# Linear attention beside softmax attention on one core: the start-up order, the guard's last operations and a new table for the order of work

## The chip, the cores and the metric

One core of a Trainium2 chip runs the whole program. The metric is the device time of one execution in microseconds; the time of a kernel is the median of several executions. A separate execution is profiled, and its span runs from the first to the last recorded instruction, so it is a little shorter than that execution's device time.

## The reference

Two independent attention blocks, A and B, each on 2048 tokens of width 512 with 32 heads of 16. A is linear attention with the feature map phi, B is full softmax attention. Their outputs lie side by side in the last dimension.

```python
def _A_ref(x, wqkv, wo):
    q, k, v = ...                       # x @ wqkv, 32 heads of 16
    phi = lambda t: jnp.where(t > 0, t + 1, jnp.exp(t)) + 1e-6
    pq, pk = phi(q), phi(k)
    kv = jnp.einsum("bhsd,bhse->bhde", pk, v)
    z = jnp.einsum("bhsd->bhd", pk)
    num = jnp.einsum("bhqd,bhde->bhqe", pq, kv)
    den = jnp.einsum("bhqd,bhd->bhq", pq, z)[..., None] + 1e-6
    return (num / den) ... @ wo

def _B_ref(x, wqkv, wo):
    q, k, v = ...
    scores = jnp.einsum("bhqd,bhkd->bhqk", q, k) * Dh ** -0.5
    o = jnp.einsum("bhqk,bhkd->bhqd", softmax(scores, axis=-1), v)
    return o ... @ wo

return concatenate([a, b], axis=-1)     # bfloat16, 1 x 2048 x 1024
```

## The kernel before

**What the bulk of the work is.** Block B has 32 heads times 2048 by 2048 scores. The kernel cuts them into 32 units (`NU`: four groups of heads, four spans of 512 queries, and the even or odd heads of the group), and each unit into 64 blocks of 128 keys by 512 queries (`UB`), 2048 blocks in all. A block needs one score matmul on PE (`qk`, L871), an exponential, and the product with V (L1129). The exponential can be done in two ways. In the first, ACT does it: two or three blocks lie in a PSUM tile `pS`, and one ACTIVATE at L1048 writes them to `PT` in 16 bits; V is then multiplied once. In the second, DVE and POOL do it with integers: the block lies in one of two banks of the PSUM tile `pD`, DVE scales and shifts it into an integer that read as a 16-bit float is close to the exponential (L956, tile `DI`), POOL adds two constants to it for two blocks at a time (L980), which makes two more shifted versions, and V is multiplied three times, with three scaled copies of V, so that the errors of the approximation cancel. This text calls the first an ACT block and the second a D block.

**Everything else** is inserted between: projections of B (`proj_job`, `v4_job`), the whole of block A (`akv_job`, `akvsum_job`, `aq_job`, `aden_job`, `anum_job`, `omm_job`), and the closing of each unit (`unit_done`).

**What sets the order.** All instructions of the four engines lie in one fixed order, which a planner in the Python program works out when the kernel is built. It keeps a planned time for each engine (`T`), a list of ready candidates with planned durations, and takes at each step the candidate with the earliest planned start; near ties go by priority, to which a random number from a seeded generator may be added. Nineteen parameters steer it, `NAMES`; one row of the table `POLICY` holds their values for 8 us of planned PE time (`SEG`), and there are 86 rows. `DBL`, the eighth, bounds the planned backlog of DVE and POOL above which no further D block is taken; `AQ`, the eighteenth, holds back the exponentials of block A; `SEED` is the fifteenth. How many of the 2048 blocks become D blocks is no constant: it comes out of this process. Dependencies between engines become semaphore waits (`Sched.add`), derived from named resources that each operation reads and writes.

**The port's turn.** A resource named `"PORT"` keeps some operations of DVE and POOL from overlapping. POOL's operations at L980 and L1191 read it; some DVE operations with two SBUF inputs write it (the phi stages at L699 and L700, the V copies at L686). Each side waits for the other's semaphore. In the plan such an operation is marked as locked, from the `keys` of its function, and starts only when POOL is planned to be free. `both` makes one planned operation of several instructions and takes the `keys` of the first.

**The guard.** `flag_job` (from L650) bounds the largest possible score: three small reductions, three matmuls, one reduction (L661), and then three operations on single numbers, L663 to L665, that leave a flag in `FLG`. The flag decides whether a general softmax has to run, which it does not for these inputs. In the plan each of the three is 0.1 us long and not locked, and none writes `"PORT"`.

**The denominators of A.** `aden_job` (from L743) plans two halves of eight matmuls at 0.0625 us for each.

**The start.** Before the planner begins, an order written by hand runs: 28 warm-up matmuls (L1206), then for each of the first four token tiles a transpose on PE (four matmuls, L570, into bank t of `SBANKS`) and a copy to `xTb` (L563, by DVE for tiles 0 and 2, by ACT for 1 and 3). The two x loads for tiles 0, 1 and 2, 3 are issued on the SP and the ACT queue. `first_proj` (L1219) is a projection for half a span, 256 tokens, of four matmuls; `first_k` (L1224) writes its result into `KM` for even or odd heads. The first half of K (bank `SBANKS[4]`) is projected in the loop, after tile 1 and before the transposes of tiles 2 and 3; then follow the two halves of Q (banks of `pD`, copies at L1237 and L1239) and the second half of K. After that the planner takes over from fixed planned times (`T` is 7.8, DVE 8.9).

Of the kernel before, what the change touches and what calls it, by code (L numbers as in the profile page):

```python
# [13 lines left out]
ALU = mybir.AluOpType  # L14
# [218 lines left out]
def bass_concat_heads__linear_attn_block__softmax_full_mha__prompt_kernel(nc, A_x, A_wqkv, A_wo, B_x, B_wqkv, B_wo, out):  # L233
# [7 lines left out]
    SC = 0.25  # L241
# [13 lines left out]
        (0.15, 3.5, 4.2, 0, 3, 5, 32, 3.0, 1.0, 16, 10.0, 0.0, 0, 0, 633, 1, 0.0, 0.0, 2.0),  # L255
        (0.05, 3.5, 4.2, 0, 3, 4, 32, 3.0, 1.0, 16, 10.0, 0.0, 1.5, 0, 0, 1, 0.0, 0.0, 2.0),
        (0.15, 3.5, 4.2, 0, 3, 5, 32, 3.0, 1.0, 16, 10.0, 0.0, 0, 0, 275, 1, 0.0, 0.0, 2.0),
        (0.05, 3.5, 4.2, 0, 3, 4, 32, 3.0, 1.0, 16, 10.0, 0.0, 1.5, 0, 0, 1, 0.0, 0.0, 2.0),
        (0.05, 3.5, 4.2, 0, 3, 4, 20, 3.0, 1.0, 16, 40.0, 0.0, 1.5, 0, 497, 1, 0.0, 0.0, 2.0),
        (0.15, 3.5, 3, 0, 3, 4, 32, 3.0, 1.0, 16, 10.0, 0.0, 0, 0, 503, 1, 0.0, 0.0, 2.0),  # L260
        (0.15, 3.5, 3, 0, 3, 4, 20, 3.0, 1.0, 16, 10.0, 0.0, 0, 0, 503, 1, 0.0, 0.0, 2.0),
        (0.15, 3.5, 4.2, 0, 3, 4, 32, 3.0, 1.0, 16, 10.0, 0.0, 0, 0, 0, 1, 0.0, 0.0, 2.0),
        (0.15, 3.5, 3, 0, 3, 4, 20, 3.0, 1.0, 16, 10.0, 0.0, 0, 0, 503, 1, 0.0, 0.0, 2.0),
        (0.15, 3.5, 4.2, 0, 3, 4, 32, 3.0, 1.0, 16, 10.0, 0.0, 0, 0, 0, 1, 0.0, 0.0, 2.0),
        (0.15, 3.5, 3, 0, 3, 4, 20, 3.0, 1.0, 16, 10.0, 0.0, 0, 0, 138, 1, 0.2, 0.0, 2.0),
        (0.15, 3.5, 3, 0, 3, 7, 20, 3.0, 1.0, 16, 10.0, 0.0, 0, 0, 313, 1, 0.2, 0.0, 2.0),
        (0.15, 3.5, 3, 0, 3, 7, 20, 3.0, 1.0, 16, 10.0, 0.0, 0, 0, 313, 1, 0.2, 0.0, 2.0),
        (0.15, 3.5, 3, 0, 3, 4, 32, 3.0, 1.0, 16, 10.0, 0.0, 0, 0, 155, 1, 0.0, 0.0, 2.0),
        (0.15, 3.5, 3, 0, 3, 4, 32, 3.0, 1.0, 16, 10.0, 0.0, 0, 0, 155, 1, 0.0, 0.0, 2.0),
        (0.15, 3.5, 4.2, 0, 3, 4, 32, 3.0, 1.0, 16, 10.0, 0.0, 0, 0, 0, 1, 0.0, 0.0, 2.0),  # L270
        (0.15, 3.5, 3, 0, 3, 4, 32, 3.0, 1.0, 16, 10.0, 0.0, 0, 0, 155, 1, 0.0, 0.0, 2.0),
        (0.15, 3.5, 3, 0, 3, 4, 32, 3.0, 1.0, 16, 10.0, 0.0, 0, 0, 9, 1, 0.0, 0.0, 2.0),
        (0.15, 2.05, 4.2, 0, 3, 4, 32, 3.0, 1.0, 16, 20.0, 0.0, 0, 0, 0, 1, 0.0, 0.0, 2.0),
        (0.15, 2.05, 4.2, 0, 3, 4, 32, 3.0, 1.0, 16, 20.0, 0.0, 0, 0, 222, 4, 0.0, 0.0, 2.0),
        (0.15, 3.5, 3, 0, 3, 4, 32, 3.0, 1.0, 16, 10.0, 0.0, 0, 0, 166, 1, 0.0, 0.0, 2.0),
        (0.15, 3.5, 3, 0, 3, 4, 32, 3.0, 1.0, 16, 10.0, 0.0, 0, 0, 166, 1, 0.0, 0.0, 2.0),
        (0.15, 3.5, 4.2, 0, 3, 4, 32, 3.0, 1.0, 16, 10.0, 0.0, 0, 0, 841, 1, 0.0, 0.0, 2.0),
        (0.15, 3.5, 4.2, 0, 3, 4, 32, 3.0, 1.0, 16, 10.0, 0.0, 0, 0, 625, 1, 0.0, 0.0, 2.0),
        (0.15, 3.5, 2.6, 0, 3, 4, 32, 3.0, 1.0, 16, 10.0, 0.0, 0, 0, 166, 1, 0.0, 2.0, 2.0),
        (0.15, 3.5, 2.6, 0, 3, 4, 32, 3.0, 1.0, 16, 10.0, 0.0, 0, 0, 166, 1, 0.0, 2.0, 2.0),  # L280
        (0.15, 3.5, 2.6, 0, 3, 4, 32, 3.0, 1.0, 16, 10.0, 0.0, 0, 0, 166, 1, 0.0, 2.0, 2.0),
        (0.15, 3.5, 2.6, 0, 3, 4, 32, 3.0, 1.0, 16, 10.0, 0.0, 0, 0, 166, 1, 0.0, 2.0, 2.0),
        (0.15, 3.5, 2.6, 0, 3, 4, 32, 3.0, 1.0, 16, 10.0, 0.0, 0, 0, 549, 1, 0.0, 2.0, 2.0),
        (0.15, 4.5, 2.6, 0, 3, 4, 32, 3.0, 1.0, 16, 40.0, 0.0, 0, 0, 889, 1, 0.0, 2.0, 2.0),
        (0.15, 3.5, 2.6, 0, 3, 4, 32, 3.0, 1.0, 16, 10.0, 0.0, 0, 0, 549, 1, 0.0, 2.0, 2.0),
        (0.15, 3.5, 4.2, 0, 3, 4, 32, 3.0, 1.0, 16, 10.0, 0.0, 0, 0, 0, 1, 0.0, 0.0, 0.3),
        (0.15, 3.5, 2.6, 0, 3, 4, 32, 3.0, 1.0, 16, 10.0, 0.0, 0, 0, 549, 1, 0.0, 2.0, 2.0),
        (0.15, 3.5, 4.2, 0, 3, 4, 32, 3.0, 1.0, 16, 10.0, 0.0, 0, 0, 0, 1, 0.0, 0.0, 2.0),
        (0.15, 3.5, 2.6, 0, 3, 4, 32, 3.0, 1.0, 16, 10.0, 0.0, 0, 0, 549, 1, 0.0, 2.0, 2.0),
        (0.15, 3.5, 4.2, 0, 3, 4, 32, 3.0, 0.2, 16, 10.0, 0.0, 0, 0, 916, 1, 0.0, 2.0, 2.0),  # L290
        (0.15, 3.5, 2.6, 0, 3, 4, 32, 3.0, 1.0, 16, 10.0, 0.0, 3, 0, 863, 1, 0.0, 2.0, 2.0),
        (0.15, 3.5, 2.6, 0, 3, 4, 32, 3.0, 1.0, 16, 10.0, 0.0, 3, 0, 13, 1, 0.3, 2.0, 2.0),
        (0.15, 2.5, 4.2, 0, 3, 4, 32, 3.0, 1.0, 16, 10.0, 0.0, 0, 0, 851, 1, 0.0, 0.0, 2.0),
        (0.15, 2.5, 4.2, 0, 3, 4, 32, 3.0, 1.0, 16, 10.0, 0.0, 0, 0, 851, 1, 0.0, 0.0, 2.0),
        (0.15, 3.5, 2.6, 0, 3, 4, 32, 3.0, 1.0, 16, 10.0, 0.0, 3, 0, 63, 1, 0.2, 2.0, 2.0),
        (0.15, 3.5, 2.6, 0, 3, 4, 32, 3.0, 1.0, 16, 10.0, 0.0, 3, 0, 63, 1, 0.2, 2.0, 2.0),
        (0.15, 3.5, 2.6, 0, 3, 4, 32, 3.0, 1.0, 16, 10.0, 0.0, 3, 0, 63, 1, 0.2, 2.0, 2.0),
        (0.15, 3.5, 2.6, 0, 3, 4, 32, 3.0, 1.0, 16, 10.0, 0.0, 3, 0, 172, 1, 0.2, 2.0, 2.0),
        (0.15, 3.5, 2.6, 0, 3, 4, 32, 3.0, 1.0, 16, 10.0, 0.0, 3, 0, 500, 1, 0.3, 2.0, 2.0),
        (0.15, 3.5, 4.2, 0, 3, 4, 32, 3.0, 1.0, 16, 10.0, 0.0, 0, 1.5, 820, 1, 0.0, 0.0, 2.0),  # L300
        (0.15, 3.5, 4.2, 0, 3, 4, 32, 3.0, 1.0, 16, 10.0, 0.0, 0, 1.5, 820, 1, 0.0, 0.0, 2.0),
        (0.15, 3.5, 2.6, 0, 3, 4, 32, 3.0, 1.0, 16, 10.0, 0.0, 3, 0, 1, 1, 0.3, 2.0, 2.0),
        (0.15, 3.5, 4.2, 0, 3, 4, 32, 3.0, 1.0, 16, 10.0, 0.0, 0, 0, 0, 1, 0.0, 0.0, 2.0),
        (0.15, 3.5, 6, 0, 2, 4, 32, 3.0, 1.0, 16, 10.0, 0.0, 3, 0, 1, 1, 0.3, 2.0, 2.0),
        (0.15, 3.5, 6, 0, 2, 4, 32, 3.0, 1.0, 16, 10.0, 0.0, 3, 0, 1, 1, 0.3, 2.0, 2.0),
        (0.15, 3.5, 4.2, 0, 3, 4, 32, 3.0, 1.0, 16, 10.0, 0.0, 0, 0, 530, 1, 0.0, 0.0, 0.3),
        (0.15, 3.5, 6, 0, 2, 4, 32, 3.0, 1.0, 16, 10.0, 0.0, 3, 0, 1, 1, 0.3, 2.0, 2.0),
        (0.05, 3.5, 6, 0, 2, 4, 32, 3.0, 1.0, 16, 10.0, 0.0, 3, 0, 525, 1, 0.3, 2.0, 4.0),
        (0.15, 3.5, 6, 0, 2, 4, 32, 3.0, 1.0, 16, 10.0, 0.0, 3, 0, 1, 1, 0.3, 2.0, 2.0),
        (0.15, 3.5, 2.6, 0, 2, 4, 32, 3.0, 1.0, 16, 10.0, 0.0, 3, 0, 996, 1, 0.3, 0.0, 2.0),  # L310
        (0.15, 3.5, 4.2, 0, 3, 4, 32, 3.0, 1.0, 16, 10.0, 0.0, 0, 0, 0, 1, 0.0, 0.0, 2.0),
        (0.15, 3.5, 4.2, 0, 3, 4, 32, 3.0, 1.0, 16, 10.0, 0.0, 0, 0, 0, 1, 0.0, 0.0, 2.0),
        (0.25, 3.5, 2.6, 0, 2, 4, 32, 6.0, 1.0, 16, 10.0, 0.0, 0.5, 0, 996, 1, 0.3, 0.0, 2.0),
        (0.25, 4.5, 2.6, 0, 2, 4, 32, 6.0, 0.2, 16, 10.0, 0.0, 0.5, 0, 996, 1, 0.0, 0.0, 2.0),
        (0.25, 4.5, 2.6, 0, 2, 4, 32, 6.0, 0.2, 16, 10.0, 0.0, 0.5, 0, 996, 1, 0.0, 0.0, 2.0),
        (0.25, 4.5, 2.6, 0.1, 2, 4, 32, 9.0, 1.0, 16, 10.0, 0.0, 0.5, 0, 684, 1, 0.3, 0.0, 2.0),
        (0.25, 4.5, 2.6, 0, 2, 4, 32, 6.0, 0.5, 16, 10.0, 0.0, 0.5, 0, 829, 1, 0.0, 0.0, 2.0),
        (0.25, 4.5, 2.6, 0.1, 2, 4, 32, 9.0, 1.0, 16, 10.0, 0.0, 1.5, 0, 883, 1, 0.3, 0.0, 2.0),
        (0.25, 4.5, 2.6, 0, 2, 4, 32, 6.0, 0.5, 16, 10.0, 0.0, 3, 0.5, 231, 1, 0.0, 0.0, 2.0),
        (0.25, 4.5, 2.6, 0, 2, 4, 32, 6.0, 0.5, 16, 10.0, 0.0, 3, 0.5, 231, 1, 0.0, 0.0, 2.0),  # L320
        (0.25, 4.5, 2.6, 0, 2, 4, 32, 6.0, 0.5, 16, 10.0, 0.0, 3, 0.5, 231, 2, 0.0, 0.0, 4.0),
        (0.25, 4.5, 2.6, 0, 2, 4, 32, 6.0, 0.5, 16, 10.0, 0.0, 3, 0.5, 231, 2, 0.0, 1.0, 4.0),
        (0.25, 4.5, 2.6, 0, 2, 4, 32, 6.0, 0.5, 16, 10.0, 0.0, 1.5, 0.5, 553, 1, 0.0, 0.0, 2.0),
        (0.25, 4.5, 2.6, 0, 4, 4, 32, 6.0, 0.5, 16, 10.0, 0.0, 3, 0.5, 231, 2, 0.0, 1.0, 4.0),
        (0.25, 4.5, 2.6, 0, 4, 4, 32, 6.0, 0.5, 16, 10.0, 0.0, 3, 0.5, 231, 2, 0.0, 1.0, 4.0),
        (0.15, 3.5, 3, 0, 3, 4, 32, 9.0, 1.0, 16, 10.0, 0.0, 0, 0, 0, 2, 0.0, 0.0, 2.0),
        (0.25, 4.5, 2.6, 0, 4, 4, 32, 6.0, 0.5, 16, 10.0, 0.0, 3, 0.5, 251, 2, 0.0, 1.0, 2.0),
        (0.15, 3.5, 3, 0.1, 3, 4, 32, 9.0, 1.0, 16, 10.0, 0.0, 0, 0, 0, 2, 0.45, 0.0, 2.0),
        (0.15, 3.5, 3, 0, 3, 4, 32, 9.0, 1.0, 16, 40.0, 0.0, 0, 0, 0, 2, 0.0, 0.0, 2.0),
        (0.25, 3.5, 3, 0, 3, 4, 32, 9.0, 1.0, 16, 40.0, 0.0, 0, 0, 701, 2, 0.0, 0.0, 2.0),  # L330
        (0.25, 3.5, 3, 0, 3, 4, 32, 9.0, 1.0, 16, 40.0, 0.0, 0, 0, 701, 2, 0.0, 0.0, 2.0),
        (0.5, 3.5, 3, 0, 3, 4, 32, 6.0, 1.0, 24, 40.0, 0.0, 0, 0, 0, 2, 0.0, 0.0, 2.0),
        (0.25, 3.5, 3, 0, 3, 5, 32, 9.0, 1.0, 16, 40.0, 0.0, 0, 0, 928, 2, 0.0, 0.0, 2.0),
        (0.15, 3.5, 4.2, 0, 3, 4, 32, 3.0, 1.0, 16, 10.0, 0.0, 0, 0, 259, 1, 0.0, 0.0, 2.0),
# [14 lines left out]
    with es:  # L349
# [25 lines left out]
        PQT = sb("PQT", [128, 1, 4, 512], BF)  # L375
# [852 lines left out]
        for t in range(4):  # L1228
# [4 lines left out]
            if t == 1:  # L1233
                first_proj(SBANKS[4], 1, 0)
# [304 lines left out]
```

## Time and profile before

| what | before |
|---|---|
| median of 6 runs | 704.26 us (701.69 to 704.92) |
| the profiled execution, device time | 703.66 us |
| its span | 701.8 us |
| mean granted TensorE clock | 0.998 |
| busy: PE, ACT, DVE, POOL | 666.2, 681.2, 573.1, 579.9 us |
| ACT blocks: ACTIVATEs on three and on two blocks | 291 and 290, which is 1453 blocks |
| D blocks: score matmuls into `pD` at L871 | 595 |
| POOL's operation for two D blocks, L980 | 1890 ns mean |
| first exponential (L1048) starts, last ends | 10.87 us, 692.96 us |

The times are microseconds from the first instruction. ACT is busy 97% of the span. A busy PE is not a PE at its peak, since the records of pipelined matmuls overlap. Device time and span of the profiled execution differ by 1.9 us; the span and the median by 2.5 us.

### The profile page before, as it was taken

The page shows a single profiled execution, that of the slowest core. Times are in us where ns is not written, and L with a number is a line of the kernel's source. Part 1 is how long each engine was busy: PE and PEld are TensorE (multiplying, and loading weights), DVE is VectorE, ACT ScalarE, POOL GpSimd, SP SyncE. Part 2 cuts the span into 40 slices and gives each one's busy share as a digit, 9 for nine tenths or more (in the row PEclk, how much of TensorE's full clock was granted, in tenths as well). Part 3 has the DMA queues.
Part 4 walks back from the last instruction along what each step waited for, and adds up shares of the span by engine and source line. Part 5 has one row for each costly group of instructions (what it writes and reads, how often), then busy time and mean ns, then how long its engine had stood idle before and what let it go on. Part 6 is the DMA issues. An engine that isn't in the chain of part 4 may idle for free.

```text
span 701.8 us, 15842 instructions
## 1 busy us (share of the span) xinstructions
PE 666.2 (95%) x6740; PEld 226.3 (32%) x6740; DVE 573.1 (82%) x1022; ACT 681.2 (97%) x637; POOL 579.9 (83%) x350
## 2 busy tenths in 40 slices
PE   7999998999999999999999999999999999999996
PEld 5333443333333334332222223332222222322221
DVE  4878889888788888888888888978889888887873
ACT  5799999999999999999999999999999999999995
POOL 6398666787888887896899879987789987998993
PEclk9999999999999999999999999999999999999999
DMA  9900000000000000010000000000010000101001
GB/s 208 243 1 3 2 1 4 8 14 9 2 2 1 2 1 2 1 40 16 18 23 23 9 1 16 24 24 9 15 30 18 16 16 25 24 23 38 17 24 34
DMA packets 35788, 17.34 MB, mean 25 GB/s; under 512 B 26496, under 2 KB 35200, under 8 KB 35712
## 3 DMA queue, kind: packets, MB, share of 16 engines
q1 hardware_dynamic: 34480, 15.48, 9.3%
q8 instruction: 55, 0.90, 0.5%
q10 hardware_dynamic: 1232, 0.79, 0.4%
q14 instruction: 21, 0.17, 0.1%
HBM read 4.72 MB, written 4.19 MB: 13 GB/s over the span
## 4 chain that ended last, share of the span: by engine, by line
ACT 80%; PE 11%; DVE 5%; POOL 3%; issue 0%; ACTq 0%; POOLq 0%
ACT PT L1048 77%; PE pPV L1129 4%; PE pS L871 2%; POOL DI L980 2%; ACT EA L697 2%; DVE DI L956 2%; PE pD L871 1%; PE pD L787 1%; PE pD L677 1%; PE pD L708 1%; PE pD L1206 0%; PE pD L595 0%; DVE KM L608 0%; DVE VV L686 0%; DVE KNa L700 0%
## 5 line engine op out<-in xcount | busy, mean ns | idle before, releaser
L1048 ACT ACTIVATE PT<-pS 128x1536 f16<-128x1536 f32 x581 | 667.6, 1337 | 5.9 <-PE pD L871 3.5
L980 POOL TENSOR_TENSOR DI<-DI,SHC 128x1024 int32<-128x1024 int32 x298 | 555.4, 1890 | 99.1 <-DVE DI L956 46.3
L956 DVE TENSOR_SCALAR DI<-pD 128x512 int16<-128x512 f32 (+1 forms) x588 | 391.8, 691 | 70.8 <-PE pD L871 59.4
L1129 PE MATMUL pPV<-DI,VV 128*17 128x512 f16 x1785 | 245.7, 381 | 0.9 <-DVE OT L1184 0.7
L1129 PE MATMUL pPV<-PT,VV 128*17 128x512 f16 x1453 | 241.5, 382 | 1.6 <-ACT PT L1048 1.1
L871 PE MATMUL pS<-QT,KM 32*128 32x512 bf16 x1453 | 226.0, 384 | 16.3 <-ACT PT L1048 11.3
L871 PE MATMUL pD<-QT,KM 32*128 32x512 bf16 x595 | 211.7, 384 | 5.1 <-DVE DI L956 3.6
L871 PEld LDWEIGHTS pS<-QT,KM 32*128 32x128 bf16 x1453 | 55.4, 91 | 193.5 <-ACT PT L1048 146.1
L1129 PEld LDWEIGHTS pPV<-DI,VV 128*17 128x17 bf16 x1785 | 52.4, 88 | 70.7 <-issue 52.2
L871 PEld LDWEIGHTS pD<-QT,KM 32*128 32x128 bf16 x595 | 51.5, 90 | 65.6 <-DVE DI L956 40.8
L1129 PEld LDWEIGHTS pPV<-PT,VV 128*17 128x17 bf16 x1453 | 51.6, 88 | 59.1 <-issue 42.8
L708 PE MATMUL pD<-Wa,xTa 128*128 128x128 bf16 x512 | 36.7, 220 | 1.1 <-DVE DI L956 0.8
L595 PE MATMUL pD<-xTb,Wb 128*128 128x512 bf16 x120 | 33.0, 383 | 0.4 <-DVE VV L682 0.2
L708 PEld LDWEIGHTS pD<-Wa,xTa 128*128 128x128 bf16 x512 | 28.8, 98 | 12.7 <-DVE DI L956 7.7
L1191 POOL TENSOR_TENSOR OT<-OT,ZR 128x256 bf16<-128x256 f32 x31 | 19.3, 621 | 10.3 <-DVE KNa L700 4.7
L1184 DVE STREAM_TRANSPOSE OT<-pPV 128x512 f32<-128x512 f32 x31 | 22.0, 709 | 2.7 <-PE pPV L1129 2.6
L677 PE MATMUL pD<-Wb,xTb 128*128 128x128 bf16 x256 | 18.5, 220 | 0.4 <-DVE DI L956 0.4
L711 DVE CAST KNa<-pD 128x256 bf16<-128x256 f32 x32 | 13.4, 419 | 6.5 <-PE pD L708 6.5
L735 PE MATMUL pD<-xTa,Wa 128*128 128x512 bf16 x64 | 17.8, 383 | 0.3 <-DVE DI L956 0.3
L787 PE MATMUL pD<-WOa,ONT 128*128 128x512 bf16 x64 | 18.0, 383 | 0.0
L697 ACT ACTIVATE EA<-KNa 128x256 bf16<-128x256 bf16 x32 | 15.4, 481 | 1.2 <-DVE KNa L711 1.2
L677 PEld LDWEIGHTS pD<-Wb,xTb 128*128 128x128 bf16 x256 | 14.4, 98 | 6.7 <-DVE DI L956 3.8
(106 smaller groups left out, 303.0 us busy)
## 6 DMA issues: line engine op xcount, KB each, us to landing
out_dram<-OB SPq DMA_DIRECT2D x16, 128.0 KB, 1.7
out_dram<-KNa SPq DMA_DIRECT2D x13, 128.0 KB, 1.7
Wa<-in_A_wqkv_dram SPq DMA_DIRECT2D x1, 1536.0 KB, 7.3
KM<-KR SPq DMA_DIRECT2D x96, 16.0 KB, 1.8
Wb<-in_B_wqkv_dram SPq DMA_DIRECT2D x2, 384.0 KB, 4.1
Wb<-in_B_wqkv_dram SPq DMA_DIRECT2D x1, 512.0 KB, 4.9
WOa<-in_A_wo_dram SPq DMA_DIRECT2D x1, 512.0 KB, 8.0
VNa<-in_B_wo_dram SPq DMA_DIRECT2D x1, 512.0 KB, 4.3
```

Of the source, the lines that this page charges most:

```text
L595: return e.matmul(f32v(bk), lhsT=Wb[:, cc, kind * 512 + Gp * 128:kind * 512 + Gp * 128 + 128], rhs=xTb[:, cc, sc * 512:(sc + 1) * 512], st ...
L677: return e.matmul(f32v(bk)[:, tl * 128:(tl + 1) * 128], lhsT=xTb[:, cc, t * 128:(t + 1) * 128], rhs=Wb[:, cc, 1024 + Gp * 128:1024 + Gp * ...
L697: ("act", 0.051 + n * 0.000833, f_op("act", lambda e: e.activation(EA[:, q, 0:n], t_ap, ACTF.Exp), list(keys), [("EA", q)])),
L708: return e.matmul(f32v(bk)[:, 128 * x:128 * x + 128], lhsT=xTa[:, cc, (t + i_) * 128:(t + i_ + 1) * 128], rhs=Wa[:, cc, c0:c0 + 128], star ...
L787: return e.matmul(f32v(bk), lhsT=src, rhs=WO[:, hb, :], start=(hb == 0), stop=(hb == 3))
L871: return e.matmul(dst, lhsT=KM[32 * g:32 * g + 32, Gp % 2, e_, j * 128:(j + 1) * 128], rhs=QT[32 * g:32 * g + 32, Gp % 2, c * 512:(c + 1) ...
L956: sch.add("dve", lambda e: e.tensor_scalar(DI[:, buf, 0, i * 512:(i + n) * 512], DB[:, bi * 512:(bi + n) * 512], ESC, EB, op0=ALU.mult, op ...
L980: sch.add("pool", lambda e: e.tensor_tensor(DI32[:, buf, 1:3, 0:w], DI32[:, buf, 0, 0:w].unsqueeze(1).broadcast_to([128, 2, w]), SHC32[:]. ...
L1048: sch.add("act", lambda e: e.activation(PT[:, row, c0:c0 + w], SCR[sl][:, 0:w], ACTF.Exp, scale=SC), reads=skeys(sl), writes=[("PT", row, ...
L1129: sch.add("pe", lambda e, g=g, vk=vk, c0=c0, P=P, first=first, last_=last_: e.matmul(PVb[32 * g:32 * g + 17, 0:512], lhsT=VV[:, Gp % 2, vk ...
L1184: sch.add("dve", lambda e: e.transpose(OT[:, 0, :], PVb[:, 0:512]), reads=[("PV", g) for g in range(4)], writes=[("OT", 0)])
L1191: (ml, 0.65, f_op(ml, lambda e: e.tensor_tensor(xn[:, :, 16 * e_:16 * e_ + 16], o[:, :, 0:16], zr.unsqueeze(2).broadcast_to([128, 16, 16]) ...
```

## The change

It has four parts. All four transposes of the start are issued before the first projection of half of K; before, that projection stood between the second and the third. The guard's last three operations become one planned operation of 0.5 us, each of them writes `"PORT"`, and so the whole is locked and each waits for POOL, and POOL for them. The planned duration of one matmul in `aden_job` is 0.03 us where it was 0.0625. And the table `POLICY` has 86 new rows; one row, by position, is the same as before, and the rows in which `DBL` is above 3.0 are 31 where they were 21.

```diff
     POLICY = [
-        (0.15, 3.5, 4.2, 0, 3, 5, 32, 3.0, 1.0, 16, 10.0, 0.0, 0, 0, 633, 1, 0.0, 0.0, 2.0),
-        (0.05, 3.5, 4.2, 0, 3, 4, 32, 3.0, 1.0, 16, 10.0, 0.0, 1.5, 0, 0, 1, 0.0, 0.0, 2.0),
...
         (0.15, 3.5, 4.2, 0, 3, 4, 32, 3.0, 1.0, 16, 10.0, 0.0, 0, 0, 0, 1, 0.0, 0.0, 2.0),
+        (0.25, 3.5, 4.2, 0, 3, 4, 20, 3.0, 1.0, 16, 10.0, 0.0, 0, 0, 0, 1, 0.0, 0.0, 1.0),
+        (0.25, 3.5, 3, 0, 3, 4, 20, 3.0, 0.5, 16, 10.0, 0.0, 0, 0, 0, 1, 0.0, 0.0, 1.0),
...
-                ("dve", 0.1, f_op("dve", lambda e: e.tensor_tensor(GR1[:, 3:4], GR1[:, 1:2], GR1[:, 2:3], op=ALU.mult), ["GR1"], ["GR2"])),
-                ("dve", 0.1, f_op("dve", lambda e: e.scalar_tensor_tensor(GR1[:, 2:3], GR1[:, 0:1], SC * SC, GR1[:, 0:1], op0=ALU.mult, op1=ALU.mult), ["GR1", "GR2"], ["GR1"])),
-                ("dve", 0.1, f_op("dve", lambda e: e.tensor_tensor(FLG[:], GR1[:, 3:4], GR1[:, 2:3], op=ALU.mult), ["GR1", "GR2"], ["FLG"]))],
+                ("dve", 0.5, both(
+                    f_op("dve", lambda e: e.tensor_tensor(GR1[:, 3:4], GR1[:, 1:2], GR1[:, 2:3], op=ALU.mult), ["GR1"], ["GR2", "PORT"]),
+                    f_op("dve", lambda e: e.scalar_tensor_tensor(GR1[:, 2:3], GR1[:, 0:1], SC * SC, GR1[:, 0:1], op0=ALU.mult, op1=ALU.mult), ["GR1", "GR2"], ["GR1", "PORT"]),
+                    f_op("dve", lambda e: e.tensor_tensor(FLG[:], GR1[:, 3:4], GR1[:, 2:3], op=ALU.mult), ["GR1", "GR2"], ["FLG", "PORT"])))],
...
-            return Job(halves(f, [("PQT", 0, bq) for bq in range(4)] + [("RHZ", bq) for bq in range(4)], n=16, parts=2, dur=0.0625) + [
+            return Job(halves(f, [("PQT", 0, bq) for bq in range(4)] + [("RHZ", bq) for bq in range(4)], n=16, parts=2, dur=0.03) + [
...
             tok[("xTb", t)] = 6.0
-            if t == 1:
-                first_proj(SBANKS[4], 1, 0)
+        first_proj(SBANKS[4], 1, 0)
         first_k(SBANKS[4], 0, 0, fk(0))
         first_proj(DBANK[0], 0, 0)
```

## The prediction

> **What bounds the kernel now.** I read the page first: busy shares, then the costliest groups.
>
> ```profile
> PE 666.2 (95%) x6740; PEld 226.3 (32%) x6740; DVE 573.1 (82%) x1022; ACT 681.2 (97%) x637; POOL 579.9 (83%) x350
> ...
> ACT 80%; PE 11%; DVE 5%; POOL 3%; issue 0%; ACTq 0%; POOLq 0%
> ...
> L1048 ACT ACTIVATE PT<-pS 128x1536 f16<-128x1536 f32 x581 | 667.6, 1337 | 5.9 <-PE pD L871 3.5
> L980 POOL TENSOR_TENSOR DI<-DI,SHC 128x1024 int32<-128x1024 int32 x298 | 555.4, 1890 | 99.1 <-DVE DI L956 46.3
> ```
>
> ACT sets the time: busy 97%, 80% of the chain that ended last, and before its 581 exponentials it idled only 5.9 us in all. One ACT block costs 667.6 / 1453 = 0.46 us of ACT. So three things can move the end: the time before the first exponential (10.87 us), idle time of ACT between the first and the last (692.96 us), and the number of ACT blocks; what follows the last, 701.8 - 692.96 = 8.8 us, the change does not edit. Idle time of DVE and POOL (18% and 17%) costs nothing unless it becomes D blocks.
>
> The second view is ACT's waits, which say where its idle time lies.
>
> ```profile
> ACT xTb L563 <- PE pS L570: 4.3, 2, 2.3
> ACT PT L1048 <- PE pD L871: 3.5, 3, 1.5
> ACT KNa L563 <- PE pD L814: 2.5, 1, 2.5
> ACT PT L1048 <- PE pS L871: 2.2, 1, 2.2
> ACT L452 <- issue: 1.9, 1, 1.9
> ACT EA L697 <- DVE KNa L711: 1.2, 1, 1.2
> ```
>
> In the timeline the inner gaps are 2.18 us before 19.96, 1.51 before 28.44, 1.18 before 117.10 and 0.59 before 672.52: 5.46 us. The rest of the list is the head and the tail.
>
> **The start.** The third view is the timeline of the first 11 us.
>
> ```profile
> 4.57 1.04 PE L570 MATMUL pS<-identb,ON 128*128 128x128 bf16 x8
> 5.65 0.60 ACT L563 ACTIVATE xTb<-pS 128x512 bf16<-128x512 bf16 x1 [2.29 <-PE pS L570]
> 6.30 1.04 PE L1219 MATMUL pS<-xTb,Wb 128*128 128x256 bf16 x4 [0.69 <-ACT xTb L563]
> 7.13 1.06 PE L570 MATMUL pS<-identb,ON 128*128 128x128 bf16 x8
> 7.98 1.93 PE L1219 MATMUL pD<-xTb,Wb 128*128 128x256 bf16 x8
> 9.95 0.42 DVE L1239 CAST QT<-pD 128x256 bf16<-128x256 f32 x1 [1.33 <-PE pD L1219]
> 10.87 6.91 ACT L1048 ACTIVATE PT<-pS 128x1536 f16<-128x1536 f32 x6 [1.41 <-PE pD L871]
> ```
>
> PE ends the first eight transposes at 5.61 and stands 0.69 us until ACT has copied tile 1 (6.25). After the change the other eight matmuls of the transposes fill that hole: 5.61 to 6.65. They need the second x load. It was issued at 0.81 with the first, the two took 3.7 and 4.1 us to land by the page's DMA part, so it is there at 4.9. The transposes and the half projection follow each other at 0.83 us (6.30 to 7.13) and 0.85 (7.13 to 7.98), so the first K half starts at 6.65, the two Q halves at 7.48 and, 1.93 us for both, end at 9.41. Tile 3, which the second Q half needs, is copied by ACT from 6.69 to 7.29, ahead of that. The Q copy that releases the first scores therefore starts near 9.45 where it was 9.95: **0.5 us gained**, and DVE, whose copy of tile 2 moves from 7.80 to 6.2, has nothing in its way. Behind the moved projection in PE's queue stand both Q halves; the move puts no DMA into another place, and SP and POOL have nothing to do with it. The bounds: nothing, if the new order meets the early gap at 19.96 anyway, and 0.69, the whole hole. Below nothing is excluded as long as the load lands before 5.61.
>
> The row for the clock: here a half projection has 273 to 421 ns a matmul and a transpose about 130 ns from one to the next (1.04 / 8), and later in the run 128-column matmuls go eight in 0.62 us; yet the page's granted clock is 9 tenths or more in every slice, the first too. The Trainium skill, "TensorE: Matmul & The Clock Gate", Part 1, says that the array runs at half speed until a free-running window of about 3.4 us was busy throughout, and that a hole in the work can void the window. By that rule the closed hole could bring full speed a window earlier, some 1.2 us more (an estimate, half of three half projections of 0.83), or, with the window elsewhere, leave more of the start at half speed and give back about 0.2. The sum leaves this out.
>
> **The guard.** The fourth view is DVE, with POOL beside it, around 114 us.
>
> ```profile
> 112.20 3.74 POOL L980 TENSOR_TENSOR DI<-DI,SHC 128x1024 int32<-128x1024 int32 x2 [1.40 <-DVE DI L956]
> ...
> 113.23 0.87 DVE L663 TENSOR_TENSOR GR<-GR 1x1 f32<-1x1 f32 x1
> 114.14 1.82 DVE L664 SCALAR_TENSOR_TENSOR GR<-GR 1x1 f32<-1x1 f32 x1
> 115.99 0.15 DVE L665 TENSOR_TENSOR FLG<-GR 1x1 f32<-1x1 f32 x1
> ```
>
> Three operations on one number should cost the same; L665, with POOL idle, took 0.15 us. L663 ended at 114.10 and L664 at 115.96, each as a POOL operation ended (112.20 + 1.87 = 114.07, and 115.94). So POOL held them up, and 0.87 + 1.82 - 2 x 0.15 = 2.4 us of DVE were lost. Behind them stood the D evictions and a K copy of A (L711, 116.66) for which ACT waited 1.18 us, and POOL then stood 2.72 us before 118.67. Now the three are placed when POOL is planned free, 3 x 0.15 = 0.45 us against 0.5 planned. The added wait: POOL's next L980 is queued behind the last of the three and starts up to 0.5 us late; POOL is 83% busy, so the products with its shifted blocks come 0.5 us later, which six `DI` buffers cover (without them it would be 0.5 us of ACT). The added wait in the other direction: if the real POOL is late against the plan, DVE stands at the head of its queue for up to one L980, 1.89 us, with the evictions behind it, as it does now. So the gain lies between 0 and 1.18; I take **1.18**, as the wait has a named owner.
>
> **The planned length of the denominators' matmuls.** Eight of them take 0.36 us in the trace (338.31 to 338.67, the last one's flight included); planned were 8 x 0.0625 = 0.50, now 0.24. The device does the same work. The plan gains 8 halves x 0.26 = 2.1 us of PE. In 325 to 350, where two of them lie, ACT is busy 25.00 of 25 us, so this can pay only as D blocks. Bounds 0 and 2.1 (and -0.4, four denominators by 0.1, should the plan now be short by 0.36 - 0.24 each); I take 0.3.
>
> **The new order.** No row shows it, so it is bounded by what an order can change. First the inner gaps left, 5.46 - 1.18 = 4.28 us: an order could remove all or make as many again. The two large ones lie in the first 30 us, when DVE works through 0.74 us K evictions and 0.69 us V copies with PE waiting for banks; I take a quarter to a third of 4.28 as removed, **1.2 us**. Second the split. The unevenness shows in POOL:
>
> ```profile
> 75.00:100.00 25.00, 24.07 (x304) 11.55 (x304) 21.53 (x45) 24.90 (x26) 15.68 (x9) 1.00 0.01 2
> 375.00:400.00 25.00, 24.50 (x224) 6.92 (x222) 20.79 (x34) 25.00 (x24) 24.64 (x15) 1.00 0.05 14
> 400.00:425.00 25.00, 22.60 (x235) 6.99 (x231) 22.34 (x39) 25.00 (x25) 18.25 (x12) 1.00 0.01 2
> ```
>
> The fifth busy column is POOL: 9 operations in one stretch of 25 us, 15 in another. One pair of blocks more or fewer is worth 2 x 0.46 = 0.92 us of ACT. A shift of five pairs either way is 4.6 us. More rows with a larger `DBL` let more D blocks be taken, fewer rows with `AQ` above 0 (8 against 27) let A's exponentials in at once; neither tells a number, so I take 0 for the split.
>
> **The sum:** 0.5 + 1.18 + 0.3 + 1.2 = 3.2 us. The profiled span goes from 701.8 to 698.6; against the median of 704.26, with the same 2.5 us between them, that is **701.0 us**. Its own range is 699 to 703.
>
> **The rivals.** *A larger share for DVE and POOL:* ten more D blocks, 701.0 - 4.6 = 696.4 us. For it: POOL idles 99 us before L980. Against it: PE is at 95%, and a D block needs three products with V where an ACT block needs one. *The gain is swallowed:* the start and the guard are mended, but the planner's fixed starting times do not move, and the new order opens gaps as large as those closed; 0.5 + 1.18 less 1.6 of new gaps, about 704.2 us. It includes the case that the start does nothing, the second load being late. For it: a gap of 2.18 at 19.96 can absorb all that the start gains. *Slower, by the split:* the new order gives DVE and POOL fewer D blocks, since another way through the plan fills the port with two-input operations at other places. Price 0.46 us a block: 14 fewer are 6.4 us, less the 1.7 of start and guard, 709.0 us. It decides from 4 fewer (1.7 / 0.46), and is visible from 9 fewer. For it: 24.5 and 17.3 us of POOL's idle time already end at the two-input operations L700, so the pairs depend on their places. Against it: ACT's inner gaps of under 1% show that plan and device agree, so an order planned shorter should be shorter.
>
> **How the numbers follow.** Forecast 0.42, larger share 0.12, swallowed 0.20, slower 0.26. A difference of 0.3%, 2.1 us, is about what the runs can tell, so the borders are 702.15 and 706.37. Four fifths of the forecast (0.34), the larger share (0.12) and a little of the third are faster: 0.48. The rest of the forecast, most of the third and the small end of the fourth stay within: 0.26. Slower: 0.26. The range takes the gains with half the larger share on one side, and on the other the lower half of the slower case: 697.0 to 707.5.
>
> **What would show it.** The first exponential at 10.4 us (10.87 now), eight transposes directly behind the first eight; L663 to L665 at 0.15 us each with no POOL operation over them, and no ACT wait at L697 of about 1 us; score matmuls into `pD` at 595 with a few either way, ACT's exponentials near 667 us; inner gaps of ACT near 3 us. It is wrong if L871 into `pD` falls below 587 or ACT's inner idle time rises above 7 us.

## The result, and the profile after

| what | before | after |
|---|---|---|
| median | 703.26 us (85 runs, 701.59 to 705.42) | 701.17 us (42 runs, 699.76 to 702.96) |
| ratio to before | | 0.9972, 95% interval 0.9967 to 0.9978 |
| profiled execution: device time, span | 703.66, 701.8 us | 699.87, 698.0 us |
| ACT blocks and D blocks | 1453 and 595 | 1458 and 590 |
| first exponential | 10.87 us | 8.43 us |

The changed kernel is 2.1 us faster, just under the 0.3% taken as the border, and clear of noise. The profiled pair differs by 3.8 us; why that is more is explained below. From here on L numbers of the changed kernel are one higher than before's between the guard and the moved call (L872 is the score matmul, L957 and L981 the D path, L1049 the exponential).

The page of the changed kernel, busy shares and costliest groups:

```profile
PE 665.6 (95%) x6735; PEld 225.7 (32%) x6735; DVE 567.0 (81%) x1017; ACT 682.6 (98%) x639; POOL 574.9 (82%) x347
...
ACT 87%; PE 8%; DVE 2%; POOL 1%; DMA 1%; issue 0%; ACTq 0%
...
L1049 ACT ACTIVATE PT<-pS 128x1536 f16<-128x1536 f32 x583 | 669.5, 1343 | 3.8 <-PE pS L872 1.8
L981 POOL TENSOR_TENSOR DI<-DI,SHC 128x1024 int32<-128x1024 int32 x295 | 550.5, 1891 | 100.0 <-DVE DI L957 32.8
```

ACT is still the bound and does more than before: five more blocks, 669.5 us of exponentials against 667.6. POOL has three operations fewer. So the gain is not in the split; it must be idle time of ACT. The timeline of ACT shows all its gaps between the first exponential and the last (start, length of the stretch, and in brackets the idle time before it):

```profile
8.43 6.89 ACT L1049 ACTIVATE PT<-pS 128x1536 f16<-128x1536 f32 x6 [0.98 <-PE pD L872]
16.98 2.37 ACT L1049 ACTIVATE PT<-pS 128x1536 f16<-128x1536 f32 x2 [1.66 <-PE pS L872]
19.68 49.93 ACT L1049 ACTIVATE PT<-pS 128x1536 f16<-128x1536 f32 x44 [0.34 <-PE pD L872]
129.32 1.45 ACT L1049 ACTIVATE PT<-pS 128x1536 f16<-128x1536 f32 x1 [0.37 <-issue]
289.25 2.37 ACT L1049 ACTIVATE PT<-pS 128x1024 f16<-128x1024 f32 x2 [0.18 <-PE pD L872]
635.77 53.43 ACT L1049 ACTIVATE PT<-pS 128x1536 f16<-128x1536 f32 x47 [0.16 <-PE pS L872]
```

The inner gaps are 1.66 + 0.34 + 0.37 + 0.18 + 0.16 = 2.7 us; they were 5.46. There is none near 115 us any more. The guard, on DVE and then POOL:

```profile
109.59 0.15 DVE L664 TENSOR_TENSOR GR<-GR 1x1 f32<-1x1 f32 x1
109.77 0.15 DVE L665 SCALAR_TENSOR_TENSOR GR<-GR 1x1 f32<-1x1 f32 x1
109.95 0.15 DVE L666 TENSOR_TENSOR FLG<-GR 1x1 f32<-1x1 f32 x1
```

```profile
106.94 1.89 POOL L981 TENSOR_TENSOR DI<-DI,SHC 128x1024 int32<-128x1024 int32 x1
110.18 1.89 POOL L981 TENSOR_TENSOR DI<-DI,SHC 128x1024 int32<-128x1024 int32 x1 [1.34 <-DVE FLG L666]
```

Three operations of 0.15 us; POOL's operation before them ended at 108.8, and the one after waits for the last of them, as the edit orders. Then the start, on PE:

```profile
4.68 1.07 PE L570 MATMUL pS<-identb,ON 128*128 128x128 bf16 x16
5.99 0.61 PE L1220 MATMUL pS<-xTb,Wb 128*128 128x256 bf16 x4 [0.24 <-DVE xTb L563]
6.44 1.04 PE L1220 MATMUL pD<-xTb,Wb 128*128 128x256 bf16 x8
```

All sixteen matmuls of the transposes took 1.07 us, where eight took 1.04 before, and the two Q halves 1.04 where they took 1.93. That is twice the speed, from the first transpose on, and the edit comes after that point. So this part of the 3.8 us needs a test of its own.

### The profile page after: what moved, and what is told of

Its sections match the earlier page's. It is cut to its first block, busy times and chain, and to the rows that moved or that the text cites. A ratio compares the mean times of both kernels' runs of the same rounds, so it can differ in the third digit from the quotient of the medians.

```text
span 698.0 us, 15831 instructions
## 1 busy us (share of the span) xinstructions
PE 665.6 (95%) x6735; PEld 225.7 (32%) x6735; DVE 567.0 (81%) x1017; ACT 682.6 (98%) x639; POOL 574.9 (82%) x347
## 4 chain that ended last, share of the span: by engine, by line
ACT 87%; PE 8%; DVE 2%; POOL 1%; DMA 1%; issue 0%; ACTq 0%
ACT PT L1049 85%; PE pPV L1130 3%; ACT EA L698 2%; PE pS L872 2%; DVE DI L957 1%; PE pD L872 1%; POOL DI L981 1%; PE pD L678 1%; PE pD L595 1%; DMA ON<-in_B_x_dram 1%; PE pD L709 1%; PE pD L788 0%; ACT KNa L563 0%; DVE KNa L701 0%; PE pD L806 0%
## 5 line engine op out<-in xcount | busy, mean ns | idle before, releaser
L1049 ACT ACTIVATE PT<-pS 128x1536 f16<-128x1536 f32 x583 | 669.5, 1343 | 3.8 <-PE pS L872 1.8
L981 POOL TENSOR_TENSOR DI<-DI,SHC 128x1024 int32<-128x1024 int32 x295 | 550.5, 1891 | 100.0 <-DVE DI L957 32.8
L957 DVE TENSOR_SCALAR DI<-pD 128x512 int16<-128x512 f32 x583 | 387.8, 690 | 68.5 <-PE pD L872 58.1
L1130 PE MATMUL pPV<-DI,VV 128*17 128x512 f16 x1770 | 256.8, 381 | 1.2 <-DVE OT L1185 0.9
L1130 PE MATMUL pPV<-PT,VV 128*17 128x512 f16 x1458 | 251.0, 382 | 1.3 <-ACT PT L1049 1.2
L872 PE MATMUL pS<-QT,KM 32*128 32x512 bf16 x1458 | 227.1, 384 | 14.1 <-ACT PT L1049 9.1
L872 PE MATMUL pD<-QT,KM 32*128 32x512 bf16 x590 | 211.4, 384 | 3.7 <-DVE DI L957 2.6
L872 PEld LDWEIGHTS pS<-QT,KM 32*128 32x128 bf16 x1458 | 55.7, 91 | 194.1 <-ACT PT L1049 144.4
L1130 PEld LDWEIGHTS pPV<-DI,VV 128*17 128x17 bf16 x1770 | 55.4, 88 | 69.1 <-issue 49.5
L1130 PEld LDWEIGHTS pPV<-PT,VV 128*17 128x17 bf16 x1458 | 54.9, 88 | 60.3 <-issue 43.3
L872 PEld LDWEIGHTS pD<-QT,KM 32*128 32x128 bf16 x590 | 51.4, 90 | 62.6 <-DVE DI L957 39.1
L709 PEld LDWEIGHTS pD<-Wa,xTa 128*128 128x128 bf16 x512 | 28.8, 98 | 12.3 <-DVE DI L957 6.1
```

The source lines that it names most:

```text
L709: return e.matmul(f32v(bk)[:, 128 * x:128 * x + 128], lhsT=xTa[:, cc, (t + i_) * 128:(t + i_ + 1) * 128], rhs=Wa[:, cc, c0:c0 + 128], star ...
L872: return e.matmul(dst, lhsT=KM[32 * g:32 * g + 32, Gp % 2, e_, j * 128:(j + 1) * 128], rhs=QT[32 * g:32 * g + 32, Gp % 2, c * 512:(c + 1) ...
L957: sch.add("dve", lambda e: e.tensor_scalar(DI[:, buf, 0, i * 512:(i + n) * 512], DB[:, bi * 512:(bi + n) * 512], ESC, EB, op0=ALU.mult, op ...
L981: sch.add("pool", lambda e: e.tensor_tensor(DI32[:, buf, 1:3, 0:w], DI32[:, buf, 0, 0:w].unsqueeze(1).broadcast_to([128, 2, w]), SHC32[:]. ...
L1049: sch.add("act", lambda e: e.activation(PT[:, row, c0:c0 + w], SCR[sl][:, 0:w], ACTF.Exp, scale=SC), reads=skeys(sl), writes=[("PT", row, ...
L1130: sch.add("pe", lambda e, g=g, vk=vk, c0=c0, P=P, first=first, last_=last_: e.matmul(PVb[32 * g:32 * g + 17, 0:512], lhsT=VV[:, Gp % 2, vk ...
```

## The experiments

All ratios are to the kernel before, on the same chip in the same session. The first four change one thing in one of the two kernels and leave the order of all later instructions as it was.

**The start alone**, in the kernel before:

```diff
-            if t == 1:
-                first_proj(SBANKS[4], 1, 0)
+        first_proj(SBANKS[4], 1, 0)
```

> The kernel before with the start alone changed: all four transposes, then the half projections; table and planner untouched, so all later instructions keep their order. Theory A (the hole of 0.69 us is filled at the speed seen before): first exponential near 10.4 us, ratio to before 0.9993. Theory B (closing the hole also lets PE reach its full clock earlier): first exponential between 8.4 and 9.5 us in most executions, ratio near 0.9975. Theory C (the early gap of ACT at 20 us absorbs whatever the start gains): first exponential earlier by either amount, but the gap before the exponential near 20 us longer by as much, ratio 1.000.

Measured: 702.54 us, 0.9993 (0.9981 to 1.0005). ACT's timeline:

```profile
8.63 6.88 ACT L1048 ACTIVATE PT<-pS 128x1536 f16<-128x1536 f32 x6 [0.97 <-PE pD L871]
17.63 6.97 ACT L1048 ACTIVATE PT<-pS 128x1536 f16<-128x1536 f32 x6 [2.11 <-PE pS L871]
26.11 9.29 ACT L1048 ACTIVATE PT<-pS 128x1536 f16<-128x1536 f32 x8 [1.51 <-PE pD L871]
```

The gaps are 2.11 and 1.51 us, before's were 2.18 and 1.51. Nothing of the start is absorbed, and theory C falls. The ratio fits A and does not fit B, though the first exponential stands at 8.63. The ratio shows less than the start is worth, however: 10 of these 12 executions have a mean granted clock of 0.996 or less, which goes with a spell of half clock later in the run (last section), against 11 of 32 of the kernel before in the same session.

**The old start in the changed kernel**, the same edit undone there:

```diff
+            if t == 1:
+                first_proj(SBANKS[4], 1, 0)
-        first_proj(SBANKS[4], 1, 0)
```

> The changed kernel with the old start: the half projection of K again between the second and the third transpose, all else as in the changed kernel. Ratio of the changed kernel to before is 0.9972. Theory A: 0.5 us are lost, 0.9979. Theory B: 1.5 to 2 us are lost, 0.9995 to 1.000. Theory C: nothing is lost, 0.9972.

Measured: 701.12 us, 0.9965 (0.9953 to 0.9976). By the interval B is out, and A's 0.9979 lies just outside too: by the times, taking the new start away cost nothing. But the nine executions lie within 0.73 us of each other, and eight of them have a granted clock of 0.997 or more, where only 23 of 44 of the changed kernel have; among executions with such a clock the medians are 701.12 and 700.44. The profile tells more. PE at its start:

```profile
4.61 0.62 PE L570 MATMUL pS<-identb,ON 128*128 128x128 bf16 x8
5.92 0.61 PE L1220 MATMUL pS<-xTb,Wb 128*128 128x256 bf16 x4 [0.69 <-ACT xTb L563]
6.36 0.61 PE L570 MATMUL pS<-identb,ON 128*128 128x128 bf16 x8
6.81 0.60 PE L1220 MATMUL pD<-xTb,Wb 128*128 128x256 bf16 x4
7.66 0.61 PE L1220 MATMUL pD<-xTb,Wb 128*128 128x256 bf16 x4 [0.25 <-ACT xTb L563]
```

The hole of 0.69 us is there, and PE runs at full speed before and after it. So the hole does not bring down a start that already has full speed. What it does to one that is still at half speed this profile can't tell.

**The hole filled with idle work**, in the kernel before: six matmuls that nobody reads.

```diff
             if t == 1:
+                def hole(e):
+                    for i_ in range(6):
+                        ins = e.matmul(f32v(DBANK[0], 128), lhsT=identb[:], rhs=identb[:], start=True, stop=True)
+                    return ins
+                sch.add("pe", hole, reads=["identb"], writes=[DBANK[0][3]])
                 first_proj(SBANKS[4], 1, 0)
```

> The kernel before with six matmuls that nobody reads put into the hole of PE before the first half projection; order and table otherwise untouched. Theory A (only the reordering of real work gains): ratio 1.000 to 1.0003, first exponential at 10.9 us. Theory B (the hole keeps the clock down): the projections after it run at about half their time, first exponential near 9.5 us in most executions, ratio 0.998 to 0.9985.

Measured: 703.46 us, 0.9995 (0.9982 to 1.0008). No gain that can be seen, but B's upper end, 0.9985, lies inside the interval, so the times leave it open. Its one profile has the first exponential at 9.73, after a start whose first half ran at half speed and whose second at full, which by itself can't tell a cause from chance. The old start just shown had its full speed before the hole and does not test B; the other starts that began at half speed do (below).

**The guard alone**, in the kernel before: one-input operations in place of the three (the flag is then not the product).

```diff
-e.tensor_tensor(GR1[:, 3:4], GR1[:, 1:2], GR1[:, 2:3], op=ALU.mult)
+e.tensor_scalar(GR1[:, 3:4], GR1[:, 1:2], 1.0, None, op0=ALU.mult)
-e.scalar_tensor_tensor(GR1[:, 2:3], GR1[:, 0:1], SC * SC, GR1[:, 0:1], op0=ALU.mult, op1=ALU.mult)
+e.tensor_scalar(GR1[:, 2:3], GR1[:, 0:1], SC * SC, None, op0=ALU.mult)
-e.tensor_tensor(FLG[:], GR1[:, 3:4], GR1[:, 2:3], op=ALU.mult)
+e.tensor_scalar(FLG[:], GR1[:, 2:3], 1.0, None, op0=ALU.mult)
```

> The kernel before with the guard's last three operations made one-input operations on the same numbers (the flag is then no longer the product), in the same order and with the same planned times: nothing can be held up by POOL there. Theory: each takes about 0.15 us, the 1.18 us gap of ACT before 117 us is gone, ratio 0.9983. Rival: the 2.4 us of DVE come back, but ACT meets another wait within a few us (PE is at 95%), and the ratio stays at 1.000 within 0.0004.

Measured: 702.15 us, 0.9977 (0.9964 to 0.9990). DVE, then ACT, around the guard:

```profile
111.40 0.19 DVE L663 TENSOR_SCALAR GR<-GR 1x1 f32<-1x1 f32 x1
111.62 0.20 DVE L664 TENSOR_SCALAR GR<-GR 1x1 f32<-1x1 f32 x1
111.86 0.20 DVE L665 TENSOR_SCALAR FLG<-GR 1x1 f32<-1x1 f32 x1
```

```profile
107.08 6.99 ACT L1048 ACTIVATE PT<-pS 128x1024 f16<-128x1024 f32 x6
113.78 0.59 ACT L697 ACTIVATE EA<-KNa 128x256 bf16<-128x256 bf16 x1
```

They run while POOL works (two operations, 110.36 to 114.10) and cost 0.2 us each; ACT goes from the exponentials into A's without a gap. The rival is out: the interval lies below 1.

**What the table is worth.** Four kernels break the fit between table and plan, each at another place.

The changed kernel with the table of before (`POLICY` replaced by the old 86 rows, all else changed):

> The changed kernel with the table of before: new start, new planned times, no new table. Theory D (the table is worth little net, start and guard carry the gain): body between the first exponential and the last as in the changed kernel within 1 us, ratio to before 0.9965 to 0.9980, D blocks within 5 of 595. Theory E (each table fits only the plan it was searched for): the same rows steer another sequence after the guard near 110 us, ACT gaps grow, the body is 2 to 6 us longer than in the changed kernel, ratio 1.000 to 1.006.

The kernel before with the new table alone:

> The kernel before with the new table alone; the guard is planned as before, so the order is that of the changed kernel up to the guard near 110 us and another one after it. Theory D: gaps near 20 and 28 us as in the changed kernel (1.66 and 0.34 us), the rest as in before with the guard's 1.2 us, ratio 0.998 to 0.9995. Theory E: 2 to 6 us lost after the guard, ratio 1.002 to 1.008.

The changed kernel with one planned duration back:

```diff
-n=16, parts=2, dur=0.03)
+n=16, parts=2, dur=0.0625)
```

> The changed kernel with the denominators' matmuls planned at 0.0625 us again; the order is the same until the first of them near 300 us. Prediction's term: 0.3 us lost, bounds -0.4 to 2.1, ratio to before 0.9976. Theory E: the sequence after 300 us is another, not the one the table was searched for, and 1 to 4 us are lost, ratio 0.9985 to 1.003.

The changed kernel with the 15th number of each row raised by one where it was above zero:

> The changed kernel with each seed above zero raised by one, so that near ties fall otherwise in most stretches; every other parameter is the same. It shows what an order of the same parameters costs that was not picked. Theory D: within 1 us of the changed kernel, ratio to before 0.9965 to 0.998. Theory E: gaps of ACT and the number of D blocks are drawn anew, 2 to 6 us longer than the changed kernel, ratio 1.000 to 1.006, with fewer than 590 D blocks or more than 5 us of ACT idle between the exponentials.

| kernel | median | ratio (interval) | D blocks | idle before the exponentials |
|---|---|---|---|---|
| old table in the changed kernel | 731.86 us | 1.0423 (1.0407 to 1.0439) | 580 | 24.6 us |
| new table in the kernel before | 727.79 us | 1.0354 (1.0337 to 1.0370) | 580 | 20.6 us |
| denominators planned long | 722.89 us | 1.0290 (1.0276 to 1.0304) | 582 | 16.1 us |
| seeds plus one | 738.62 us | 1.0503 (1.0477 to 1.0530) | 577 | 29.2 us |

All four chose theory E, and every one lies far beyond its 2 to 6 us (1 to 4 for the third). The third is the most telling, since nothing differs on the device but the order behind the first denominators, whose matmuls start at 329.0 us in the changed kernel. ACT's waits in it:

```profile
ACT PT L1049 <- PE pD L872: 11.2, 18, 1.5
ACT PT L1049 <- PE pS L872: 4.1, 5, 1.7
ACT KNa L563 <- PE pD L815: 3.7, 1, 3.7
ACT EA L698 <- DVE PQT L739: 2.3, 3, 1.5
```

Many short waits, 18 times for a D score matmul that stands ahead of ACT's own in PE's queue, none above 1.5 us. Of its 22.9 us of span beyond the changed kernel's, 12.3 are gaps before exponentials (16.1 - 3.8), 2.3 gaps before A's, 6.8 more busy time of ACT (689.4 - 682.6; eight more ACT blocks at 0.46 are 3.7 of it), and 1.1 a longer wait in the tail (3.73 - 2.63).

**Start and guard without the new table:** the kernel before, its own table and order, with the new start, and with the guard's second factor as a per-partition scalar, so that the flag is the same product.

```diff
-e.tensor_tensor(GR1[:, 3:4], GR1[:, 1:2], GR1[:, 2:3], op=ALU.mult)
+e.tensor_scalar(GR1[:, 3:4], GR1[:, 1:2], GR1[:, 2:3], None, op0=ALU.mult)
-e.scalar_tensor_tensor(GR1[:, 2:3], GR1[:, 0:1], SC * SC, GR1[:, 0:1], op0=ALU.mult, op1=ALU.mult)
+e.tensor_scalar(GR1[:, 2:3], GR1[:, 0:1], GR1[:, 0:1], SC * SC, op0=ALU.mult, op1=ALU.mult)
-e.tensor_tensor(FLG[:], GR1[:, 3:4], GR1[:, 2:3], op=ALU.mult)
+e.tensor_scalar(FLG[:], GR1[:, 3:4], GR1[:, 2:3], None, op0=ALU.mult)
```

> The kernel before, in its own order and with its own table, with the new start and with the guard's last three operations taking one factor as a per-partition scalar, so that each has one SBUF tensor input and computes the same. Theory G (start and guard are the whole gain, the new table only repairs the order): first exponential about 0.9 us earlier at equal clock, no gap of ACT before 115 us, ratio to before 0.9970 to 0.9975, as the changed kernel. Rival (the new order gains by itself): this one gets about half, 0.998 to 0.9985.

The changed kernel itself, beside it:

> The changed kernel itself, on the same chip, for comparison: ratio to before 0.9972, and a second profile of its start. At the speed of its first profile the time from the first transpose to the first exponential is 3.75 us; if its PE is slow at the start this time, about 5.8 us.

Measured: 700.95 us, 0.9963 (0.9950 to 0.9975), and for the changed kernel 701.11 us, 0.9965 (0.9952 to 0.9978). The two are the same. Theory G holds: start and guard are the whole gain, and the rival's half is outside the interval. The three operations took 0.13 to 0.14 us here, under two POOL operations that ran from 110.60 to 114.35.

**An earlier warm-up**, added to the changed kernel and to the one just above:

```diff
+        WU = sb("WU", [128, 128], BF)
...
+        sch.add("dve", lambda e: e.memset(WU[:], 1.0), writes=["WU"])
         mk_ident(identb, "identb")
...
-            for i_ in range(28):
-                ins = e.matmul(f32v(DBANK[0], 128), lhsT=identb[:], rhs=identb[:], start=True, stop=True)
+            for i_ in range(34):
+                ins = e.matmul(f32v(DBANK[0], 128), lhsT=WU[:], rhs=WU[:], start=True, stop=True)
```

> The changed kernel with its warm-up from a tile that DVE fills first, so that PE starts near 1.0 us where it was 1.59, with 34 matmuls where it were 28. Theory F (PE reaches its full speed a certain time after it began, later in some executions than in others, and this makes the spread of the times): more executions have full speed at the first transposes; median 0.4 to 0.8 us below the changed kernel's, lowest time the same, spread smaller. Rival: the speed of the start has nothing to do with when PE begins, median within 0.3 us of the changed kernel's.

> The same kernel with the earlier warm-up added. Theories F and G together: ratio to before 0.9960 to 0.9968, below the changed kernel's. Without F: the same as without the earlier warm-up.

Measured: 701.54 us, 0.9970 (0.9956 to 0.9984), in the changed kernel, which is no gain over its 701.11; and 699.85 us, 0.9952 (0.9935 to 0.9969), in the other, 1.1 us below its pair but with overlapping intervals. PE began at 1.12 in both. In the first profile the sixteen matmuls of the transposes took 1.74 us all the same, in the second 1.05. Theory F is not shown: an earlier begin does not ensure the speed. The last kernel has the lowest median of all and may be the best version, but the intervals do not separate it from the changed kernel, and none of its seven executions has a granted clock below 0.997, where five of its pair's ten have: the spell alone may make the difference.

## Why the prediction was right, and where only the total was

**What adds up.** Two distances in the profiles separate the parts from the chance of the start: from the first transpose to the first exponential, and from there to ACT's second copy of the tail (the "body"). Full speed is the moment at which back-to-back matmuls of 128 columns start 0.06 us apart where it was 0.11 (of 256 columns, 0.11 where it was 0.21); the clock record of each trace has its first entry there.

| kernel | start order | transpose to exponential | PE at full speed from | body |
|---|---|---|---|---|
| before | old | 6.30 us | 9.97 us | 685.66 us |
| guard alone | old | 4.62 | 4.32 | 685.17, with a spell of half speed near 420 (last section) |
| hole filled | old | 5.04 | 5.69 | 686.60, with the spell |
| old start in the changed kernel | old | 4.62 | 4.54 | 684.49 |
| start alone | new | 3.75 | 4.30 | 685.57 |
| start and guard, old table | new | 4.58 | 7.14 | 685.15, with the spell |
| the same, earlier warm-up | new | 3.73 | 4.08 | 684.13 |
| changed kernel, first profile | new | 3.75 | 4.33 | 684.51 |
| changed kernel, second profile | new | 4.11 | 5.45 | 685.66, with the spell |
| changed kernel, earlier warm-up | new | 4.14 | 6.23 | 685.65, with the spell |

- **The start:** 4.62 - 3.75 = 0.87 us where full speed comes before the transposes; 0.5 was predicted, with the hole's 0.69 as the upper bound. The mechanism was right as far as it went: the eight moved transposes take 0.45 us out of the way of the Q halves (6.36 to 6.81 in the old start of the changed kernel). The bound failed because the old start has a second wait, for ACT's copy of tile 3 ahead of the second Q half, which comes 0.85 us after the first (6.81, 7.66) where four such matmuls take 0.45 (5.99 to 6.44 in the new start); at the half speed of the prediction's rows it was all but hidden (1.93 us for the eight). Where full speed comes late, the gain is larger still (see the chance of the start). That the start might do nothing is refuted by the start alone: same gaps after it. The medians by themselves do not show the start's gain; it rests on these profiles.
- **The guard:** among bodies with the spell 686.60 - 685.17 = 1.43 and 686.60 - 685.15 = 1.45 us, among those without it, both with the new start, 685.57 - 684.13 = 1.44. Predicted 1.18, the ACT gap, which was also the upper bound. The owner of the wait and the place were right, and the size was read a little short. The stretch of exponentials ahead of A's in the kernel before:

```profile
108.93 6.99 ACT L1048 ACTIVATE PT<-pS 128x1024 f16<-128x1024 f32 x6
117.10 0.42 ACT L697 ACTIVATE EA<-KNa 128x256 bf16<-128x256 bf16 x1 [1.18 <-DVE KNa L711]
```

  From start to start that is 8.17 us, and with the guard alone 6.70 (107.08 to 113.78), 1.47 less for the same six exponentials. There A's exponential starts 0.29 us before the record in front of it ends (107.08 + 6.99 = 114.07): ACT's records overlap when it does not wait, so the 1.18 us between two records cost 1.47.
- **The planned length of the denominators**, 0.3 us, can't be seen by itself: taken back without a new table it costs 22 us, which is the price of a misfit and not of the term. (Its lower bound was summed too small: eight halves by 0.12 us are 1.0 and not 0.4.)
- **The new order** was given 1.2 us of gain, and 0 for the split. This step failed. Against the old order with the guard mended, the new one's body is longer: 684.51 against 684.13, and with the spell 685.66 against 685.15; 0.4 to 0.5 us lost. The two halves can be read off the pair without the spell: its inner gaps are 2.7 us against 4.2 (2.11, 1.51 and 0.59), 1.5 gained, near the 1.2 predicted; but it has five D blocks fewer, and ACT is busy 1.7 us longer (682.6 against 680.9), 1.5 of it exponentials (669.5 against 668.0); 0.2 more are a longer wait in the tail. The term for the gaps was right, the zero for the split was wrong.

Together 0.87 + 1.44 - 0.45 = 1.9 us where full speed comes early, against the measured 2.1 of medians over executions with all kinds of starts, with and without the spell. The prediction had 3.2 us from a median of 704.26 that came from six runs; with 85 runs before's median is 703.26. The predicted 701.0 met 701.17 because the gain was taken 1.1 us too large and the starting value was 1.0 us too high: that the total fits so well is luck.

**The rivals.** "A larger share" did not occur; the share fell. "Swallowed by the gap at 20 us" is refuted, since that gap stayed at 2.11 us when the start came earlier. "Slower by the split" named a real force: five fewer blocks are one more than the four at which it was to decide, and it was only because the gaps shrank by nearly as much that it did not. Its size for an order that no one picked was far too small: the four misfits lost 20 to 36 us, not 5, more by idle time of ACT than by blocks.

**The chance of the start.** The profiled pair differs by 3.8 us and the medians by 2.1 because before's profile had its start at half speed and the changed kernel's at full; 6.30 - 4.62 = 1.68 us is what the speed is worth in the old start. The Trainium skill, "TensorE: Matmul & The Clock Gate", Part 1, states a free-running window of about 3.4 us that has to be busy, so that the moment of full speed differs from run to run; the runs here agree with the chance (the changed kernel's own two profiles differ, 4.33 and 5.45 us), though the earliest full speed came 2.7 us after PE's first matmul (1.59 to 4.30), sooner than 3.4.

The reading that the prediction hung on it, that a hole of 0.69 us might void the window (theory B of the experiments), fits the profiles. The two old starts at full speed had it before the hole, so they do not test it. Two starts met the hole at half speed, the kernel before and the new table in the kernel before, and full speed came at 9.97 and 10.39 us. In the other ten profiles PE met no such hole on the way, and it came between 4.08 and 7.36 us; seven of these too were at half speed at the first transposes. From the first transpose to the first exponential the two took 6.30 and 6.45 us, the seven 3.89 to 5.04.

The times point the same way: of 70 executions of the kernel before with the clock on record, the 48 at 0.997 or more fall into two groups, 26 from 701.60 to 702.81 us and 22 from 703.33 to 704.71, and the profiled one, 703.66, is in the second; 23 such executions of the changed kernel spread over 699.76 to 701.39 without such a gap. So what the prediction left out of its sum, some 1.2 us for full speed a window earlier, belongs in it for a part of the executions: for those the start is worth about 1.6 us or more (6.30 against 4.68 at most in the new start), not 0.5. Two profiles against ten are few; why one execution has its full speed at 4 us and another at 7 was not found.

## What to carry to other kernels

Repair a collision where it stands before the order is searched anew: the same gain came from moving one call and giving three one-number operations a scalar operand, with the order untouched. A searched order fits only the plan it was searched for; changing one planned duration and keeping the table cost 3%, so such an edit can be judged only together with its search, and the search's own worth only against the old order with the same repairs. While PE is still at half speed, do not let it stand between its first matmuls: here full speed came after 9.9 us in the two starts that met a hole of 0.69 us at half speed, and by 7.4 us in those that met none. And compare profiles of like starts, by distances between fixed points, before reading a difference of one or two microseconds.

## What the runs showed that was not expected

In five of the ten profiles of kernels whose table fits, PE ran at half its clock (0.50) for 3.4 us in the middle of the run, always near 420 us. The mean granted clock of the whole run is 0.994 to 0.996 in these five and 0.997 to 0.999 in the other five. In the second profile of the changed kernel (stretch, busy times of PE, PEld, DVE, ACT, POOL, granted clock):

```profile
412.00:418.00 6.00, 5.57 (x61) 1.78 (x61) 5.37 (x11) 6.00 (x7) 3.41 (x3) 1.00 0.02 4
418.00:422.00 4.00, 4.00 (x35) 0.94 (x34) 2.48 (x4) 3.62 (x4) 4.00 (x3) 0.57 0.00 0
422.00:426.00 4.00, 4.00 (x51) 1.88 (x53) 3.45 (x7) 3.43 (x4) 4.00 (x3) 1.00 0.18 37
```

The granted clock is 0.57 over the 4 us, a score matmul takes 0.61 us where it takes 0.39, and ACT waits 0.95 us in all just after. It lengthens the body by about 1 us (685.66 against 684.51). The first profile of the same kernel has 1.00 there. PE was busy 5.57 of the 6 us before it, in the profile without the spell as well. Sixteen 8-column matmuls of the denominators begin 1.1 to 2.0 us ahead of it in all five, and two of the four kernels that break the fit have such a spell behind another set of them (at 329.2 us with the old table, at 590.7 with the new table in the kernel before). But most sets pass without one, and the kernel with seeds plus one has a spell of 6.8 us at 519.4 with no such set in the 10 us before it; that they have a part in it is not shown. The same view grants 1.00 throughout the first 12 us, in starts of half and of full speed alike, since the record has no entry before full speed; so for the start the matmuls' spacing has to be read.

One-number operations with two SBUF tensor inputs ended only when POOL's operation did (0.87 and 1.82 us). With a constant or a per-partition scalar as the other factor they took 0.13 to 0.20 us under a running POOL operation.
